# Sixteen FFN weight loads issued from GpSimd's queue, each behind a VectorE operation, in a one-core long-convolution and SwiGLU kernel

## The chip, the cores and the metric

One core of a Trainium2 chip. The metric is the device time of one execution in microseconds. The kernel before took 284.51, 283.94 and 284.5 us in three runs, a median of 284.5.

## What is computed

The reference normalises `x` (2048 rows of 640, bf16), runs a gated long convolution on it and then a SwiGLU feed-forward network (FFN), each with a residual. Cut to what matters:

```python
k_shift = sum over t of k_pad[:, t:t + S, :] * shift_k[:, 3 - t]      # 4 taps
kv = k_shift * v
y = irfft(rfft(pad(kv)) * rfft(pad(ssm_k)))[:S] + kv * ssm_D          # per channel
h = x + layernorm(x) * y
n = layernorm(h)
out = h + (silu(n @ w_gate) * (n @ w_up)) @ w_down                    # 640 -> 1728 -> 640
```

## The kernel before, in words

The 2048 positions are cut into four blocks `j` of 512, the 640 channels into two halves `c` of 320. The transform is a product with tables on TensorE (PE): block 0 uses dense tables, blocks 1 to 3 a two-stage transform whose stages are joined by shuffles, DMAs from SBUF to SBUF (`sh...` on the way there, `rs...` on the way back). VectorE (DVE) does the tap products (`kvn`, `kva`, `kvv`, line 709), the spectral products (`m1`, `m2`, `ac`, `ci`, `kf`, line 709 too) and part of the FFN's products (`gm`). ScalarE (ACT) empties PSUM. GpSimd (POOL) does twelve small powers for LayerNorm at line 839 (`nr`), and nothing else after the start.

For blocks 1 to 3 the filter `ssm_k` mostly comes in turned: a DMA transpose from DRAM (`kraw`, line 570), a store to a scratch tensor (`kst`), and a reload in another layout (`kld`), three DMAs that wait for one another; then PE's first pass (`s1K`) reads it. LayerNorm ahead of the FFN of block 0 goes: the power `nr10` on GpSimd, a product on VectorE at line 846, the normalised rows `hn` (line 853 on VectorE, line 854 on ScalarE), a transpose on PE (line 1075), a copy out of PSUM on VectorE (line 470), and then the FFN's matmuls (line 489). It is done for two halves of block 0, so `nr10` occurs twice.

The weights come in pieces: gate and up in column ranges 0, 1 and 2, each with rows 0 to 2 and 3 to 4 of five (`wg00`, `wg03`, `wg10`, ..., `wu23`), the last 64 columns of both as `gul`, and `w_down` in five pieces `wd` and one `wdl`. Each is one DMA, issued by SyncE (SP).

The order of the work is no decision of the hardware. A table, `_PLAN`, gives for each operation its engine, its place in that engine's order, planned times, and for some transfers another operation to wait for. Each engine runs its list in order; an instruction that waits holds up everything behind it on its engine. `plan()` reads the table (its last loop is quoted here), and `emit()` turns dependencies into semaphore waits. A transfer whose kind starts with "turn" is a DMA transpose, of DRAM (`kraw`) or of SBUF (`tr`, line 1067):

```python
            if o.dma[1].startswith("turn"):
                if soft is not None:
                    o.deps.setdefault(soft, 1)
                turn = o
            elif o.eng == "pool":
                if turn is not None:
                    o.deps.setdefault(turn, 1)
                soft = o
```

So, in the order of planned times, a transfer of GpSimd waits until the last transpose ahead of it has landed, and a transpose waits for the last transfer of GpSimd. In the kernel before GpSimd has no transfers, and the rule does nothing.

The plan also picks the slots of tiles that share memory. The builder of one DMA is `dma()`, whose `eng` names the queue; `load_weights()` holds `piece()`, which the diff changes; `LE` is "sp".

Of the kernel before, what the change touches and what calls it, by code (L numbers as in the profile page):

```python
# [307 lines left out]
def bass_sequential_preLN__ssm_conv_h3__swiglu_ffn__prompt_kernel(  # L308
# [14 lines left out]
    UC = [4,4,4,0]  # L323
# [29 lines left out]
    with ExitStack() as es:  # L353
# [875 lines left out]


# [10 lines left out]
    "c-rlI2UwF=+y6O9NCMf5kw6GZNC=QH0!c`KKn4T|5W*G&5kvuJt*h?VZMC(yw^ngfTlc85b+@isYg@Hit99?ufr|f|h-kmQz23Lq_pbkS^?9!6dCs`ceeV1B`<;j9x;ViIBO)T8)&s*uXnSH$3lUCI+xfEeM<;GO"  # L1241
    "39pn09`CQ7$kYCEmY3H{i+{ZKy!`w7e{x1*yY25=pJPn=hfadW@_!z<Et@}I`&;D~EWN0a{!Z!t&i$*`i_w3t{nfFAKk)g#wI{Tz<M&Md{}S)3cw-M6q(5x`_v(o7FVNBdg%#2t;{3Pp{-eHsj;DW>^8VX%{4J}0"
    "tX9ImNv(vxq1NA){!?oGWAy**TjW3g-uqX@{Ew)K@H;gT{t4w*RrJF9|L%#~we~#j=iggI<b^2h8B;vDw6-&#or!3OipYqI=!l0{$Pf9T0K|rq4n5vb=OPib_@i*7fl-UvMw4Nb58S=L#v7hYIJw|~j(nk=ia1af"
    "qCluI;Pi*57)ihz8+v3&i9%5X^wPjqj-*I|B2h53>yZ^|c9aDcW|Rh2ZdB}vo(5jHh!37A5M}Er0RR5rgAZPLP>V*fC=TghJO|peC<?`+1n?k%8H~t;5>YZzK_)>c1*IYjvca5D$bm9pWCn7=*gRAOK5|hZ%0@Y;"
    "0J%^;%w2-YQ5iCzDpZO(piZbGs)T$yqZ;s+jB1e@@Dac`J>X-6mQ<M42L8?9H4pMhgZT>4bo3f{NrD~|Sk$1ds0)lugVJJ@4ptUV)){C3#FGQ|#V~s@ng}fph$Ii<D?p=A1;kQ`s^QrPv6P}-s4qO1pq{864M7dy"
    "bw2tKe7u3)L?fVWJeq{wMem^QXc*Mrg0m}l8H2{cRR_HBffpel!U1*yfq_uKEe0Y;hiGhQDBw{AQCFi`Xb#~1Ca}u{1_gj(7@!)4LV!6LpsE0MDB%i&k`R1}z*j5ZL0}<)OA1yxU?2vtse?G9p{9np2BOy??mlQZ"
    "8U!(o2Xre@H^3zucuxeJT2bu|Ev;N?V03G~y-^R;4-JNl#sLeRA;M08RSvZEM$5q03e+FGZUD=b5JwP15&{t>!OTf8qX|42folWQ5}_OiF-L+HH4uLUWT1wc3g(OOXdnyjBLPh_@S_JFN2B*VI8H)S0o9o>TThs^"
    "J7}aB7|I1c9cTiY43<`y#SGX_L2m=r)6iTr4=n%<^nloU0j{Nx!2q-xVqFC|4@Bz#f%WJkv=(L?jJBd}p!A(EcQv41gEpZpkneD`3w;8t?T5^30k1Bgo%vw91MZs<9nV5DV5UZhtr6Wovth=K&^`maK0_a%<!BF#"
    "ejjZ|OuPzaUXRuQUd_PlbhH%Or=jc6w*}_d08wB}!-vrkbQB!~i{t1EbP`3t3}2%&=set~qXW=$2z<T+t564w8UR~4U{LN^A-w>Xx$w4_3F`a_=K26;TaAd=3;O`ZF<@N*`s@kFmBN_Tl~)L>tpt?k^eDaz{J1~`"
    "9pQ9CPZp>$AGBTvSvSDQ_rYHUpjqe9$7aZMIYj?4`V`RE3sD_{_>KTulYxOLU^fu$M*Glb5c6U5IXZ#90$wHpSK}eW<KS^JaQY6kokU+kuHQk1=h3(59AtY9{eW%)hRb1PH39p>(KqNcI)%PRXVFD;30(otTM!?A"  # L1250
    "jM#WTpvS{I5f`Teb6sGy^#^Q6!<w54T9^s(jDy<ipo4y(&ym3VaM1rCs11a+Do}Gz$Yv2Bz5v$TRdgA~w??@T*t~~sp$q6o^Z?yK57B+}GkS!6MNc5-b)c3_pvqB5iKSSEqj5OaVja%F%fL?)jJ}I*gMQY+idYBh"
    "<1zXLJw+t=13|$ph=9r18&k0l-V1*A0e)j4$|xLz)mVjNaRQFVDflzUQh+}}zW8&%SBO7F{@4!(;C-ORU>t&JNRAbF5@7x=3dBLU75`8ihUq90ABVg(cnaw28qE9zkiCaG<2#_ytAO4`KsyItgk0}IR%fB52tR{A"
# [76 lines left out]
```

## Time and profile before

| | |
|---|---|
| Median of three runs | 284.5 us (283.94 to 284.51) |
| The profiled execution | 285.35 us |
| Span of its instructions, first to last | 283.6 us |
| Mean granted TensorE clock | 0.994 |
| DMA traffic | 43.82 MB, mean 155 GB/s |
| DMAs issued by SyncE, ScalarE, GpSimd | 188, 2, 0 |

The profiled execution lies 1.75 us above its span, for what happens before the first and after the last instruction. A row of the timeline has start and length in us, engine, line, operation, what it writes and reads, its shape and a count; "SPq" is an issue by SyncE, whose length is the time of the issue and not of the transfer. In square brackets stands how long the engine had idled and what ended that. "To landing" runs from the start of the issue to the last byte. Rows of the windows view hold busy time and number of instructions by engine.

### The profile page before, as it was taken

The page shows a single profiled execution, that of the slowest core. Times are in us where ns is not written, and L with a number is a line of the kernel's source. Part 1 is how long each engine was busy: PE and PEld are TensorE (multiplying, and loading weights), DVE is VectorE, ACT ScalarE, POOL GpSimd, SP SyncE. Part 2 cuts the span into 40 slices and gives each one's busy share as a digit, 9 for nine tenths or more (in the row PEclk, how much of TensorE's full clock was granted, in tenths as well). Part 3 has the DMA queues.
Part 4 walks back from the last instruction along what each step waited for, and adds up shares of the span by engine and source line. Part 5 has one row for each costly group of instructions (what it writes and reads, how often), then busy time and mean ns, then how long its engine had stood idle before and what let it go on. Part 6 is the DMA issues. An engine that isn't in the chain of part 4 may idle for free.

```text
span 283.6 us, 4749 instructions
## 1 busy us (share of the span) xinstructions
PE 269.8 (95%) x1691; PEld 147.5 (52%) x1709; DVE 230.2 (81%) x433; ACT 196.2 (69%) x322; POOL 18.4 (6%) x21
## 2 busy tenths in 40 slices
PE   7799988799999999999999899999999999999996
PEld 2367655254445467644444477544445675444574
DVE  3997999999999999999899999999998724042414
ACT  4168988999899879959999778968899731510100
POOL 3000030200000203000001203000001010000000
PEclk9999999799999999999999999999999999999999
DMA  6987998988967547477366452763004053000003
GB/s 176 292 298 221 235 308 258 275 279 266 315 199 218 204 125 235 80 243 209 117 186 197 117 165 66 126 214 85 0 0 175 13 68 120 0 0 2 0 0 95
DMA packets 55859, 43.82 MB, mean 155 GB/s; under 512 B 20064, under 2 KB 52379, under 8 KB 55836
## 3 DMA queue, kind: packets, MB, share of 16 engines
q1 hardware_dynamic: 55690, 43.48, 52.2%
q8 instruction: 14, 0.23, 0.4%
q14 instruction: 9, 0.07, 0.1%
q10 hardware_dynamic: 146, 0.04, 0.1%
HBM read 21.88 MB, written 4.59 MB: 93 GB/s over the span
## 4 chain that ended last, share of the span: by engine, by line
PE 83%; DMA 7%; DVE 5%; issue 3%; ACT 1%; SPq 0%; DVEq 0%; ACTq 0%
PE ps L489 82%; DVE sb L709 4%; DMA sb<-in_A_k_dram 3%; DMA sb<-in_A_ssm_k_dram 2%; DMA k_nat<-sb 1%; DMA sb<-sb 1%; ACT sb L469 0%; PE ps L1075 0%; SPq L477 0%; ACT sb L1030 0%; DVE sb L470 0%; DVE sb L1167 0%; DVE sb L1034 0%; DVE sb L1101 0%; DVEq L217 0%
## 5 line engine op out<-in xcount | busy, mean ns | idle before, releaser
L489 PE MATMUL ps<-sb 128*128 128x320 bf16 (+2 forms) x1215 | 223.4, 338 | 5.0 <-issue 1.6
L709 DVE TENSOR_TENSOR sb<-sb 128x1280 bf16<-128x1280 bf16 (+4 forms) x266 | 176.5, 726 | 5.1 <-ACT sb L469 2.7
L489 PEld LDWEIGHTS ps<-sb 128*128 128x128 bf16 (+1 forms) x1233 | 119.0, 99 | 94.7 <-issue 9.0
L469 ACT ACTIVATE sb<-ps 128x640 bf16<-128x640 f32 (+2 forms) x153 | 104.9, 737 | 28.7 <-PE ps L489 23.2
L489 PE MATMUL ps<-sb,tab 128*64 128x320 bf16 (+2 forms) x432 | 55.4, 307 | 5.6 <-ACT sb L469 1.7
L1125 ACT ACTIVATE sb<-ps 128x1024 bf16<-128x1024 f32 (+2 forms) x32 | 29.3, 920 | 29.2 <-PE ps L489 28.9
L489 PEld LDWEIGHTS ps<-sb,tab 128*64 128x64 f16 (+2 forms) x432 | 25.2, 102 | 33.6 <-issue 12.6
L709 DVE TENSOR_TENSOR sb<-ps,sb 128x1024 bf16<-128x1024 f32 (+2 forms) x20 | 19.7, 1003 | 22.1 <-PE ps L489 22.1
L839 POOL TENSOR_TENSOR stt<-stt 128x2 f32<-128x2 f32 (+1 forms) x12 | 16.3, 1356 | 210.4 <-DVE stt L835 210.4
L1030 ACT ACTIVATE sb<-ps,stt 128x320 f32<-128x320 f32 x32 | 18.4, 624 | 6.3 <-PE ps L489 4.9
L1034 DVE SCALAR_TENSOR_TENSOR sb<-sb,stt 128x320 bf16<-128x320 bf16 x32 | 16.5, 545 | 3.1 <-ACT sb L1030 2.0
L873 ACT ACTIVATE sb<-sb,stt 128x640 uint8<-128x640 bf16 x16 | 13.4, 838 | 0.2
L866 ACT ACTIVATE sb<-sb 128x640 uint8<-128x640 bf16 x16 | 11.8, 738 | 0.5 <-DMA sb<-in_A_q_dram 0.4
L1167 DVE SCALAR_TENSOR_TENSOR sb<-ps,stt,sb 128x320 bf16<-128x320 f32 x8 | 4.1, 548 | 9.8 <-PE ps L489 9.8
L891 ACT ACTIVATE sb<-sb,stt 128x640 uint8<-128x640 bf16 x12 | 9.9, 829 | 0.6 <-DVE stt L886 0.2
L854 ACT ACTIVATE sb<-sb,stt 128x640 bf16<-128x640 bf16 x8 | 7.1, 916 | 0.0
L1192 DVE SCALAR_TENSOR_TENSOR sb<-ps,stt,sb 128x640 bf16<-128x640 f32 x4 | 3.3, 876 | 3.3 <-PE ps L489 3.3
L1188 ACT ACTIVATE sb<-ps,stt 128x640 bf16<-128x640 f32 x7 | 5.5, 785 | 0.0
L607 PE MATMUL ps<-sb 128*128 128x128 bf16 (+1 forms) x24 | 4.2, 282 | 0.4 <-DMA sb<-in_A_ssm_k_dram 0.4
L607 PEld LDWEIGHTS ps<-sb 128*128 128x128 bf16 (+1 forms) x24 | 2.0, 118 | 4.1 <-DMA sb<-in_A_ssm_k_dram 2.2
L853 DVE TENSOR_SCALAR sb<-sb,stt 128x640 bf16<-128x640 bf16 x8 | 3.4, 437 | 0.6 <-DMA sb<-sb 0.5
L819 DVE BATCH_NORM_STATS2 stt<-sb 128x6 f32<-128x320 bf16 x8 | 3.5, 480 | 0.0
(30 smaller groups left out, 30.3 us busy)
## 6 DMA issues: line engine op xcount, KB each, us to landing
sb<-sb SPq DMA_DIRECT2D x72, 160.0 KB, 2.6
sb<-in_A_k_dram SPq DMA_DIRECT2D x6, 560.0 KB, 4.5
sb<-in_A_v_dram SPq DMA_DIRECT2D x8, 320.0 KB, 4.0
sb<-in_A_q_dram SPq DMA_DIRECT2D x8, 320.0 KB, 4.4
sb<-cst_den SPq DMA_DIRECT2D x8, 256.0 KB, 4.3
k_nat<-sb SPq DMA_DIRECT2D x6, 320.0 KB, 4.4
sb<-k_nat SPq DMA_DIRECT2D x6, 320.0 KB, 3.0
out_dram<-sb SPq DMA_DIRECT2D x12, 160.0 KB, 2.0
```

The costliest lines, as they stand in the source:

```text
L469: fns = {"act": lambda a: a.activation(out=dst(), in_=src(), func=ACTF.Copy), "dve": lambda v: v.tensor_copy(out=dst(), in_=src())}
L489: return lambda t: t.matmul(o(), l(), r(), start=st, stop=sp)
L607: return t.transpose(B16(pt, b // 2, (b % 2) * CW + d * 128, pr), src, V(IDN, 0, pr, 0, pr))
L709: return lambda v: v.tensor_tensor(out=o(), in0=a(), in1=b_(), op=op)
L839: P.op({"pool": 1.05}, lambda g: g.tensor_tensor(out=y, in0=va, in1=stt[:, oCO + 4:oCO + 4 + hi - lo], op=ALU.pow), c1 + [(ST, "half")], c ...
L854: "act": lambda a: a.activation(out=dst(), in_=src(), func=ACTF.Identity, scale=rs(l, j, b), bias=tmv(l, j, 3)[:, b:b + 1])},
L866: P.op({"act": act_c(D) + 0.22}, lambda a, b=b, jt=jt: a.activation(out=JU(jt), in_=V(xt, b * D, D), func=ACTF.Copy, accum_out=tmv(l, j, 4 ...
L873: P.op({"act": act_c(D) + 0.3}, lambda a, b=b, jt=jt: a.activation(out=JU(jt), in_=V(xt, b * D, D), func=ACTF.Square, bias=tmv(l, j, 5)[:, ...
L891: P.op({"act": act_c(D) + 0.3}, lambda a, b=b, jt=jt: a.activation(out=JU(jt), in_=V(xt, b * D, D), func=ACTF.Square, bias=tmv(l, j, 5)[:, ...
L1030: P.op({"act": act_c(CW, True)}, lambda a, k=k, b=b, wt=wt: a.activation(out=VF(wt, CW), in_=B32(pt, k, CW), func=ACTF.Identity, scale=tmv ...
L1034: vec(dve1(CW), lambda v, b=b, wt=wt, xv=xv: v.scalar_tensor_tensor(out=xv(), in0=xv(), scalar=tmv(0, j, 5)[:, b:b + 1], in1=VF(wt, CW), o ...
L1125: P.op({"act": act_c(n)}, lambda a: a.activation(out=dst(), in_=src(), func=ACTF.Silu), rd, wr, -1000, name=f"si{j}{i}")
```

## The change

Sixteen of the twenty weight loads go from SyncE's queue to GpSimd's. Four stay on SyncE: `wg00`, `wu00`, `wg03` and `wg13`. Each of the sixteen gets one VectorE operation to wait for, from the list `PACED` (load, which of that name, VectorE operation, which of that name). The order of all other instructions on each engine is as before. The plan's table is new as a whole; the engines of the sixteen loads, their places, the transfers that some transfers wait for, the planned times and some slots of shared tiles are what differs in it.

```diff
-                dma(subs, kb, [], cells, {"0": 1020, "1": 1036, "2": 1040}.get(nm[2:3], 1041), eng=LE, after=list(more), name=nm)
+                dma(subs, kb, [], cells, {"0": 1020, "1": 1036, "2": 1040}.get(nm[2:3], 1041), eng=LE if nm in ("wg00", "wu00", "wg03", "wg13") else "pool", after=list(more), name=nm)
...
+        PACED = [
+            ('wu03', 0, 'kvn21', 0),
+            ('wg10', 0, 'kva21', 0),
+            ('wg23', 0, 'kva21', 0),
+            ('wu10', 0, 'kf102', 1),
+            ('wu13', 0, 'kvv20', 0),
+            ('gul', 0, 'kvv20', 0),
+            ('wd', 3, 'm1o102', 0),
+            ('wg20', 0, 'm1o102', 0),
+            ('wu23', 0, 'kva21', 2),
+            ('wd', 1, 'gm01', 0),
+            ('wu20', 0, 'm1a100', 0),
+            ('wd', 2, 'ac100', 1),
+            ('gul', 1, 'ci100', 0),
+            ('wd', 0, 'm2a110', 0),
+            ('wd', 4, 'ci110', 0),
+            ('wdl', 0, 'gm05', 0),
+        ]
...
+        for a_, i_, b_, k_ in PACED:
+            o, p = named[a_][i_], named[b_][k_]
+            if p not in o.deps:
+                o.deps[p] = 2
+                p.succ.append(o)
+                o.npred += 1
```

GpSimd, from the first power of block 0's second LayerNorm on. Before, the two powers `nr10` (128x2) stand next to each other, then the power of block 1 (128x4):

```order
L839 TENSOR_TENSOR stt<-stt 128x4 [waits s_pool,s_dve]
L839 TENSOR_TENSOR stt<-stt 128x2 [waits s_dve] x2
L839 TENSOR_TENSOR stt<-stt 128x4 [waits s_dve]
L839 TENSOR_TENSOR stt<-stt 128x2 [waits s_dve] x2
```

Now, with `wu03` (the first DMA; `s_d50` is the landing of the transpose `kraw20`) and `wg10` behind it:

```order
L839 TENSOR_TENSOR stt<-stt 128x4 [waits s_pool,s_dve]
L839 TENSOR_TENSOR stt<-stt 128x2 [waits s_dve]
L477 DMA sb<-in_B_w_up_dram 128x2x512 [waits s_d50]
L839 TENSOR_TENSOR stt<-stt 128x2 [waits s_dve]
L477 DMA sb<-in_B_w_gate_dram 128x3x512 [waits s_dve]
```

`wu03` has come between the two powers, and the second can only run when `wu03` has been issued. At the end of the moved loads stand the last two `wd`, the power of block 1, and `wdl`:

```order
L477 DMA sb<-in_B_w_down_dram 128x3x640 [waits s_dve]
L477 DMA sb<-in_B_w_down_dram 128x2x640 [waits s_dve]
L839 TENSOR_TENSOR stt<-stt 128x4 [waits s_dve]
L477 DMA sb<-in_B_w_down_dram 64x640 [waits s_dve]
L839 TENSOR_TENSOR stt<-stt 128x2 [waits s_dve] x2
```

SyncE at the same place, before: three shuffles, `wdl`, the transpose `kraw21`, its store `kst21`, a copy and its reload `kld21`:

```order
L477 DMA sb<-sb 32x4x640 [waits s_act] x2
L477 DMA sb<-sb 128x1x640 [waits s_d84]
L477 DMA sb<-in_B_w_down_dram 64x640
L570 DMA_TRANSPOSE sb<-in_A_ssm_k_dram 128x4x320 [waits s_d39,s_d89]
L477 DMA k_nat<-sb 128x4x320 [waits s_d94]
L477 DMA sb<-sb 128x1280 [waits s_dve]
L477 DMA sb<-k_nat 128x1280 [waits s_d87,s_d95]
```

Now, where `s_d120` is the landing of `wdl`:

```order
L477 DMA sb<-sb 32x4x640 [waits s_act] x2
L477 DMA sb<-sb 128x1x640 [waits s_d70]
L570 DMA_TRANSPOSE sb<-in_A_ssm_k_dram 128x4x320 [waits s_d39,s_d120,s_d74]
L477 DMA k_nat<-sb 128x4x320 [waits s_d78]
L477 DMA sb<-sb 128x1280 [waits s_dve]
L477 DMA sb<-k_nat 128x1280 [waits s_d79]
```

`wdl` has left SyncE's queue, and `kraw21`, which only followed it, now waits for its landing on GpSimd's side. Sixteen issues like `wdl`'s are gone from SyncE between `kraw20` and `kraw21`.

More of the change, by code (lines that the diff above doesn't have):

```diff
@@ L1228, in bass_sequential_preLN__ssm_conv_h3__swiglu_ffn__prompt_kernel @@
             block_j(j)
+        PACED = [
[16 more added lines that the diff above has]
+        ]
+        named = {}
+        for o in P.ops:
+            named.setdefault(o.name, []).append(o)
+        for a_, i_, b_, k_ in PACED:
[4 more added lines that the diff above has]
+                o.npred += 1
         if _INFO is not None:
@@ new lines @@
+    "NB}(woLqQ@AQ5N_gc&JPpfIF{S$~j~AqkQr4GM*E6H0-e9c6$-0&;*<J}UNj?+;oShzXi~!OK@C3-ohA2NSdgK~Ik&Q8bEy^>i4ELONtb7SJF93$Z8;#UmS1K_o(yh>}n;N(Gxb<U;ANG7V+I+B{SQI&zR3Wua_T"
+    "h;mT@*e*fks0}isDpZQfP&-tC+JX=5Q4Q#`p^hj5@L_rI&_Xo+fP)`+K=a_qgm@X?ISb81J-|;ZSd9bgHK-PKfVB>2EksU;I@uF-8tM!FWP=CAV7(ZPhY=Tek_Y}3qLHW)d})iS;W-U_DMejTPk1guT~H@95OoHv"
+    "^Ux~L@eUe}hQiEPG!acflVR0h=#PN27_^K=W8f+UKbephJ|IGe><AzOVGzFoJaB?Hsb~=3Q3bJAquJ;KkQ@#%Q6VB0pr`~?l}HSklLD%8V21)OCA9dUD;RXW%C`_CL~uz!Dh4uOfQ;0GpL*y;K#uyMUf_3kGz9er"
@@ new lines @@
+    "pT+{ZZBZTIk_gu00jEe{L<5Yx%B2=ozlygTYDB%!0Ep;a$U=MYupQu+1Y_OMQqc7=>H}KWgXD7XLkOOT!9y!pwt~et&=d=~HbdVG&nWO&16<UC|7wUJ0(vU2r}l6l1Mb5B%>>Ag3A`GGrh0Ikh^7OoO<=7HSZ(lR"
+    "DHE9Efaf?g2_#d%N&;a29-07H&p>m~Tr?jz&<MVD1$@&Xg1%@a___jc?uXU_0_)JHXbo5!fVQA*!0l$RT>z*TqK#-X#5)9ihIRq=`ylcnz{?HXnFq2v;Jyh3;Mr&vSegdDO+(+I_rc-@7@q}NU!qUYGPE03e}uLp"
+    "DqaDW*P+#b*K^41OtcurXP|FkZZp_e4_;vGj}M|l=rH;MSa<{-MJJFNk44|0v*;q+N29;N%zn^01Uxl*GHL=&Bm)jvfJ9r!${cuGGyyw*1Y4hgwUvm7y)hp!HURdOz}YTPU8NxXs`A_rYYF5h0W$9Z)|EpA<U_Sp"
@@ new lines @@
+    "z`Xz}&FZO;dZ?Suu<|3&mknsvd-$;lB3%aFZ$+O28hgO2{ovmr$krstz<Z#h4(&vH(U;)!L398eLnk3G;~`gLA;KeIZ4%^kGK`%-$06495aC618eM>BZ=);d4q&(pDr*U3yDK_{&Y-W+C3Fs5Mc2?x(7YKj@m3Uw"
+    "_W^oAxEV396RM^I)MFpOb`;dybl^f0`13CGYJjyJV15{6ehBctKXA7na3c>Qtpp4{gq+NWn!AN=KrOuTasg!XA-an$qwDAqx{n^C@6i+V1A2yjf|%C=TQ&mUdm#muU@6w)a2$nWa2j3;dX~WI2k0JPy#^{`E!4*g"
+    "^c4M!yx<4I7yp6?*a!Pz5+>t4pl2`O*B89eVFQl9DjbO|*oYJHmk=cj??P;R0PyAG&k+}MFc0qqHilv`4n{I8$AbX#p-6y*_!a(PScwHlgO31*wRjlt>o!>a36On=+T;7c(OZDtRX{r%Uxip7LR9BqqzJ!+A1ZH*"
@@ new lines @@
+    "@gtD$1osCJ>tm44$3LTAkPrC!J!-&I;3x~C_!)J<?_fG+U_Ks==YnTE9D>K-`QR-Fd>Mu3p<pb)q4-@q2kJ5x-Wj#PoF2fP-hlo<$o>S#<Za05b>zkmz{gh@cgBra2=((mAh-k={1sH>24L70KzkKb$qJ~{cOb)q"
+    "0n^36^SQwInSk*^;AbPSv^zv|0(722CLD_|0B6nv@8WPgHsffVfUP(gXW~M@{uyNB2~_P=@Zt>c?KHCCBzzh8cO4j*iXGUFQ?L`ea5~Pyd6<BIfLi(ym^}s20H>~)h`ZxJ?1g*4TsKU?G{7SmP!Qo$!1k|z`DcLH"
+    "C!sYF*f<K_VW)xTUjzG(d+OmJuzwt|a||%$72hwT44eag-GS=;7UkjsT#QR`1#W}e;woGXjCqcH@e6osOb1@x08ZUSWw-=J?*TKvL*=+5uEZU1J6wxva2>A40l+m1WOgPX8U&o{1sU#%nZUt*fIwf|8~1^{`r(0i"
@@ new lines @@
+    "5Dr0u@eteu^0QHYJOI}E<DqyM4n@Q92>d=8i9Y~#$${xwh;#z5UIDyU0|H}#wHn~R4hP}!z&{xvZ3ZkRVH5B;7OH}UCj%;CsE|lt&_v+53OLRL_Kd?*AU7#^8vYPj0qq%h2}%IWXW>Pj98AX_LH2C;J-iSlLq?|J"
+    "1t<+N(gbyu2>F_c7sGpfAY3I-+eP>z;9e*E1?Cba;|mxQa)^cS9!dxNn+Z>WN7o=zk=`MMF5XwXo)cygyh&v52+~aNMF0E5wgJuF%l*noPkhsS$>ezQ#Q<l(S^w`STc}2Al{}vCH9<>sc%AaHc&{h4CyKqD-bSC{"
+    "B%+^@ypg=jw}ZdPhwA&4Zz5>~S?+(!pG8_jVvw`^#`uQ^6b7{M!{oIA1`2`lh{B~l_u1}yCSY6upF*Z?qxPjepsi=vX^$Aq%tL_}>5`ypv?f*<dn<9W*KqImeV+K%k-WXS`e=Obk-GW~@LwFTD<GLd^<UusAzAHz"
@@ new lines @@
+    "n_5O&PCG>#9QcLb1M+a%F6u7Y^1yC%CGBGxhn_&MrGG*HilL=^O37sOV$5NjWAqGq9Asq9V9J@b%p1&?%u3eJtZ7Uo>m-ZH60i=lidp+u3s~9gDeMOJZgwcg&8}i|IqTVU4v$mM*}@sb3Fg*wFELLAaL5N)`#Drr"
+    "G;a()Gx!B3Lbyz@g}+vGLUK*eSI7@uA^SpF5S*>J$oY!bm$Q?*T#_xlEa6D`{Mphv`A7U}-V?45e^aneaFgIh@E$?$ke@<Qg&&9R7Yzue1^b0`6fy*3L)wJ?Eb1ew7uzID#JeT;Lq~+l!btLdqJ#3yvNO`9%Hptk"
+    "S@*D>Dw^W9;*)T!xvtBPsMRLwZ2I@~X)01UM}1Rc*Ns#sYrfQc7_m;bmw4811NoDHmDIDoC#gx4WwZpkjm>7a3+~0Q<$3YMAsL|~CC5cV=?Ai>G89G*rTSd;N%37viY1p)EcB7|_JLCaiS%Z=nNi2M%g``YL2DSR"
@@ L1299 @@
+    "MfY$26@pqZe&Z)@jqbJlubFvMpKtp_Y^_sb>-ENO;#*M=-^w+yl`Dkb`1<RPSKNvmZj~mqVoGTBgV2gSZn21d(?V}qc%$)G-2WeaXqZp"
 )
```

97 lines of the change are left out of this document (39 added, 58 removed).

## The prediction

> **What bounds the kernel now.** I read the totals first, then the chain that ended last, then busy time by stretch, because a share over the whole span hides which engine sets the pace where the change acts.
>
> ```profile
> span 283.6 us, 4749 instructions
> PE 269.8 (95%) x1691; PEld 147.5 (52%) x1709; DVE 230.2 (81%) x433; ACT 196.2 (69%) x322; POOL 18.4 (6%) x21
> ...
> PE 83%; DMA 7%; DVE 5%; issue 3%; ACT 1%; SPq 0%; DVEq 0%; ACTq 0%
> ```
>
> TensorE is busy for 95% of the span and holds 83% of the last chain. The sixteen moved loads were issued by SyncE between 55 and 100 us. The windows view for that stretch (per row: length, then busy time and count of PE, PEld, DVE, ACT, POOL, then granted clock, DMA share, GB/s) says more:
>
> ```profile
> 55.00:60.00 5.00, 4.69 (x43) 2.52 (x43) 4.65 (x15) 4.89 (x8) 1.20 (x1) 0.85 0.92 278
> 60.00:75.00 15.00, 14.71 (x95) 7.34 (x95) 14.86 (x24) 14.57 (x24) 0.00 (x0) 1.00 0.90 278
> 75.00:90.00 15.00, 14.94 (x93) 7.58 (x94) 15.00 (x26) 13.43 (x23) 0.00 (x0) 1.00 0.69 224
> 90.00:107.00 17.00, 16.54 (x117) 9.40 (x118) 16.76 (x41) 14.06 (x25) 1.51 (x1) 1.00 0.59 183
> ```
>
> From 55 to 107 us PE lacks only 0.31 + 0.29 + 0.06 + 0.46 = 1.12 us of full time, and VectorE 0.35 + 0.14 + 0 + 0.24 = 0.73 us. Two engines are full at once, each with a fixed order. So little can be won here, and what either loses by a new wait is not made good later. The waits of PE's weight loads from 55 to 165 us (total, times, longest) name a transfer once:
>
> ```profile
> PEld ps L489 <- DMA sb<-sb: 0.4, 1, 0.4
> ```
>
> **The change part by part.** It takes sixteen issues off SyncE, puts them on GpSimd, and adds two kinds of waits: sixteen on VectorE (written in the diff) and, through the plan's rule at the end of `plan()`, waits between GpSimd's loads and SyncE's transposes. Issue time saved on SyncE (0.43 us for the first load, row below) is worth nothing by itself: no transfer that SyncE issues later stands in PE's way for more than the 0.4 us above. The VectorE gates cost nothing either, since most end about when SyncE issued the load before; the loads keep their order of need. What costs is where GpSimd, in order as well, meets the two other waits.
>
> Step 1: `wu03`, the first load on GpSimd. It must wait until the transpose `kraw20` has landed, and behind it on GpSimd stands the second LayerNorm power of block 0 (L839, `nr10`), for which VectorE waits. From the timeline (start, length, engine) and the issues view (the transpose issued at 52.78 landed 3.9 us later):
>
> ```profile
> 52.78 1.59 SPq L570 DMA_TRANSPOSE sb<-in_A_ssm_k_dram  x1
> 55.04 0.43 SPq L477 DMA_DIRECT2D sb<-in_B_w_up_dram  x1
> 52.93 0.96 POOL L839 TENSOR_TENSOR stt<-stt 128x2 f32<-128x2 f32 x1 [14.40 <-DVE stt L835]
> 56.11 1.20 POOL L839 TENSOR_TENSOR stt<-stt 128x2 f32<-128x2 f32 x1 [2.22 <-DVE stt L835]
> 155.08 3.00 POOL L839 TENSOR_TENSOR stt<-stt 128x4 f32<-128x4 f32 x1 [42.73 <-DVE stt L835]
> 57.94 0.15 DVE L846 TENSOR_TENSOR stt<-stt 128x2 f32<-128x2 f32 x1
> 58.74 0.44 DVE L853 TENSOR_SCALAR sb<-sb,stt 128x640 bf16<-128x640 bf16 x1
> 60.53 0.82 DVE L470 COPY sb<-ps 128x1280 bf16<-128x1280 bf16 x1
> 59.78 0.72 PE L1075 MATMUL ps<-sb 128*128 128x128 bf16 x10
> 61.41 1.52 PEld L489 LDWEIGHTS ps<-sb 128*128 128x128 bf16 x11 [0.31 <-DVE sb L470]
> ...
> sb<-in_A_ssm_k_dram SPq DMA_TRANSPOSE x1, 3.9
> ```
>
> The transpose and all that SyncE issues ahead of it stay where they were, so it lands at 52.78 + 3.9 = 56.7 again. Then GpSimd issues `wu03` in a time X. The trace of before has no DMA issue by GpSimd, so X is bounded: 0.43 us below (SyncE's issue of this very load), 3.00 us above (its longest instruction, at 155.08). I take X = 1.0, nearest to GpSimd's own two rows in this stretch, 0.96 and 1.20. The power then starts at 56.7 + 0.05 + 1.0 + 0.05 = 57.8 instead of 56.11, takes its 1.20 and ends at 59.0; L846 follows at 59.04 instead of 57.94. Before, 57.94 − 57.31 = 0.63 us of other VectorE work hid the power's end; that cover is used up. VectorE is late by 1.1 = X + 0.1, and so are the queued instructions behind L846, down to the copy at 60.53, for which PE's weight load at 61.41, the FFN's, had waited already (its row names L470), so PE has nothing to spare there. **Term 1: S = 1.1 us**, between 0.5 (X = 0.43) and 3.1 (X = 3.00). `wu03` itself is hidden: issued near 56.8 and landing 4.0 us later (first row below), it is there at 60.8; its first matmuls (the piece of the chain at 62.19) then start at 63.3.
>
> ```profile
> sb<-in_B_w_up_dram SPq DMA_DIRECT2D x1, 256.0 KB, 4.0
> ...
> 62.19 9.48 PE ps L489 x55
> ```
>
> The Trainium skill, "DMA: Bandwidth & Descriptors", section "Specifications", gives a first byte after about 1 us for a DMA from GpSimd and 0.6 us for one from SyncE. No run here shows it yet; by it X would be an estimated 0.43 + 0.4 = 0.83 and the sum below 2.2 us, not 2.5.
>
> The other GpSimd instruction in the stretch, the power at 92.55, gets the load `wd` (rows 11 and 12) ahead of it. It ended at 94.06 and its reader on ScalarE started at 98.09, so 4 us hide it.
>
> ```profile
> 92.55 1.51 POOL L839 TENSOR_TENSOR stt<-stt 128x4 f32<-128x4 f32 x1 [35.23 <-DVE stt L835]
> 98.09 1.13 ACT L1030 ACTIVATE sb<-ps,stt 128x320 f32<-128x320 f32 x2
> ```
>
> Step 2: `wdl`, the last load, gated by the FFN product at 97.74 (L709 from PSUM, ends 98.95). The transpose `kraw21`, which merely followed it on SyncE, must now wait until `wdl` has landed. Behind `kraw21` stand its store, the reload `kld21`, and PE's first pass over it at 111.33. Timeline and landing times:
>
> ```profile
> 97.74 1.21 DVE L709 TENSOR_TENSOR sb<-ps,sb 128x1024 bf16<-128x1024 f32 x1
> 99.80 0.60 SPq L477 DMA_DIRECT2D sb<-in_B_w_down_dram  x1
> 100.50 1.37 SPq L570 DMA_TRANSPOSE sb<-in_A_ssm_k_dram  x1
> 105.53 0.38 SPq L477 DMA_DIRECT2D k_nat<-sb  x1
> 107.96 0.35 SPq L477 DMA_DIRECT2D sb<-k_nat  x1
> 111.33 0.23 PEld L489 LDWEIGHTS ps<-sb,tab 128*128 128x128 f16 x2
> ...
> sb<-in_B_w_down_dram SPq DMA_DIRECT2D x1, 80.0 KB, 3.0
> sb<-k_nat SPq DMA_DIRECT2D x1, 320.0 KB, 2.9
> ```
>
> The gate ends at 98.95 + S = 100.05. `wdl` lands L later: 3.0 before, of which 0.60 was the issue, so L = 3.0 + (1.0 − 0.6) = 3.4, that is 103.5. `kraw21` starts there and not at 100.50: 3.0 late. It is a chain of latencies (100.50, 105.53, 107.96, landing 110.86), so `kld21` lands near 113.9. PE wants it at 111.33 + 1.1 = 112.4. **Term 2: 1.4 us** (before it had 0.47 to spare). In general the sum is S + L − 2.0 = 2X + 0.5.
>
> Sum: 1.1 + 1.4 = **2.5 us**. Against the profiled execution, 283.6 of span and 1.75 around it (285.35), that is 287.85; the median of the runs shown is 0.85 lower than that execution, so 284.5 + 2.5 = **287.0**. With X from 0.43 to 1.9, 285.9 to 288.8.
>
> **The rivals.**
> - *Only the first wait counts*: `kraw21` took 5.0 us to land while weights and shuffles ran beside it, others of its kind 3.4. Gaining 1.6 there pays term 2.
>
> ```profile
> sb<-in_A_ssm_k_dram SPq DMA_TRANSPOSE x1, 5.0
> ...
> DMA to landing us min/median/max: 3.4/4.7/5.4
> ```
>
>  The sum is S = 1.1: 285.6. For it: DMA traffic falls after `wdl`. Against: the chain's other two transfers stay. 16%.
> - *GpSimd issues slowly.* GpSimd's instructions took 0.70 us with VectorE idle (226.67: VectorE busy 0.04) and 3.00 with VectorE full.
>
> ```profile
> 226.67:227.36 0.69, 0.69 (x7) 0.50 (x6) 0.04 (x1) 0.69 (x2) 0.69 (x1) 1.00 0.00 0
> 155.08:158.08 3.00, 2.95 (x17) 1.56 (x16) 3.00 (x6) 1.62 (x3) 3.00 (x1) 1.00 0.21 65
> ...
> 67.76 1.14 SPq L477 DMA_DIRECT2D sb<-in_B_w_up_dram  x2
> ...
> sb<-in_B_w_up_dram SPq DMA_DIRECT2D x1, 480.0 KB, 6.6
> ...
> 82.48 1.89 PE L489 MATMUL ps<-sb 128*128 128x512 bf16 x8
> ```
>
>  From `wu13` (issued at 67.76) six issues lead to `wu20`, which takes 6.6 us to land and is wanted by the sixth of the eight matmuls of the row at 82.48, near 83.6. 67.76 + 6X + 6.6 passes 83.6 + S from X = 1.9 on. At X = 2.2: S = 2.3, `wu20` 1.7 late, L = 4.6, in all 2.3 + 1.7 + 4.6 − 2.0 = 6.6: 291. 12%. The Trainium skill, "SBUF — State Buffer", section "SBUF: two separate sides", speaks for this rival and so against the change: while VectorE runs a two-port operation, GpSimd cannot write the descriptors of its DMAs. By its section "Who interferes with whom", copies and scalar operations between SBUF tiles are such operations and L709's kind is not; of the rows here that is L853 alone, 0.44 us, by which X would stay an estimated 1.0 + 0.44 at most and the sum 3.4.
> - *The clock drops.* After PE had been busy 0.68 of 2 us, its granted clock fell to 0.50:
>
> ```profile
> 50.00:52.00 2.00, 0.68 (x8) 0.29 (x8) 2.00 (x5) 1.56 (x4) 0.00 (x0) 1.00 0.71 255
> 54.00:56.00 2.00, 1.71 (x11) 0.56 (x10) 2.00 (x10) 1.79 (x4) 0.00 (x0) 0.50 1.18 326
> ```
>
>  A drop of 4 us to half speed after one of the two new pauses costs 2 us more: 289.0. Each pause is under 1.5 us. 6%.
> - *Faster.* SyncE's shuffles no longer stand behind weights. If `kraw20` landed before 55.0 (so that X + 56.11's power fits ahead of 57.94) and `wdl` by 101, both waits would be covered, and of PE's 1.12 us of gaps perhaps 0.8 would close: 283.7. Against: nothing ahead of `kraw20` moves, and one wait of 0.4 us names a transfer. 7%.
> - *No change*: the gates end where SyncE issued anyway, and both added waits hide in slack that the trace does not show: 284.5. 9%.
>
> **How the numbers follow.** The forecast has 50%, the rivals 16, 12, 6, 7 and 9. A difference of 0.2% is about what a measurement of this kernel can tell from none. Slower: 50 + 16 + 12 + 6 = 84%; same 9%; faster 7%. The range goes from no change, 284.4, to the sum at X = 2.0 (S 2.1, `wu20` 0.7 late, L 4.4: 5.2), 289.7; outside are the faster case and the upper part of slow issues, some 15%.
>
> **What would show it.** In the timeline after: `wu03`'s issue on GpSimd at 56.7, L839 behind it near 57.8, VectorE idle ahead of L846 for about 1 us "until POOL"; `kraw21` near 103.5, and PE waiting over 1 us for `sb<-k_nat` near 112. Wrong it is if L839 still starts at 56.1, if PE's wait at 112 is missing, or if X is over 1.9 and the up-projection near 84 waits for its weights.

## The result, and the profile after

The changed kernel took **288.44 us** (287.23 to 290.24, four runs) against 284.5 us for the kernel before on the same chip: a ratio of 1.014, 95% interval 1.0097 to 1.0182. In a later series on one chip it was 287.34 us (ten runs) against 284.75 (27 runs): 1.0085, interval 1.0053 to 1.0116. So the loss is 2.4 to 4 us; the prediction said 2.5, at 287.0. The ratios here and below leave out executions over 1.5% above the fastest of their kernel; of the swapped kernel that is four of six, of the fourteen one and of the kernel with a brake two, the profiled one among them each time, so a wait in these three profiles is relied on only where another kernel's profile shows it too.

The page of the changed kernel, its totals and two groups of GpSimd's issues (busy time in us and mean ns of one, then the idle time before them):

```profile
span 286.2 us, 4747 instructions
PE 269.6 (94%) x1691; PEld 147.4 (52%) x1709; DVE 230.5 (81%) x433; ACT 196.0 (69%) x322; POOL 31.2 (11%) x37
...
L477 POOL DMA_DIRECT2D sb<-in_B_w_up_dram x6 | 4.7, 792 | 11.3 <-DVE sb L709 7.2
L477 POOL DMA_DIRECT2D sb<-in_B_w_down_dram x6 | 4.4, 728 | 13.9 <-DVE sb L709 9.1
```

PE's work is the same, 269.6 us against 269.8; the span has grown by 2.6 us of waiting. An issue by GpSimd takes 0.73 to 0.79 us on average in these two groups. Where PE waits, the windows of the changed kernel tell (length; then busy time of PE, PEld, DVE, ACT, POOL; clock, DMA share, GB/s):

```profile
55.00:60.00 5.00, 3.50 (x34) 1.83 (x30) 3.05 (x8) 3.47 (x7) 2.16 (x3) 0.97 0.91 226
60.00:75.00 15.00, 13.83 (x89) 6.90 (x92) 14.86 (x23) 13.76 (x22) 7.66 (x11) 1.00 0.98 298
```

From 55 to 60 us PE has 3.50 us of work instead of 4.69 and VectorE 3.05 instead of 4.65: the first wait. (The clock was 0.97 there instead of 0.85, so PE's busy time alone overstates what it lost.) From 60 to 75 PE has 13.83 instead of 14.71, while the DMA engines are busier (0.98 instead of 0.90): this was not foreseen. GpSimd and VectorE at the first place, from the timelines of the changed kernel:

```profile
56.58 0.89 POOL L477 DMA_DIRECT2D sb<-in_B_w_up_dram  x1 [4.05 <-DMA sb<-in_A_ssm_k_dram]
57.50 0.72 POOL L839 TENSOR_TENSOR stt<-stt 128x2 f32<-128x2 f32 x1
...
58.25 0.16 DVE L846 TENSOR_TENSOR stt<-stt 128x2 f32<-128x2 f32 x1 [1.38 <-POOL stt L839]
```

`wu03` waits 4.05 us for the transpose `kraw20`, holds GpSimd for 0.89, and the power `nr10` behind it ends at 58.22; VectorE has stood still for 1.38 us "until POOL". This execution had come to 47 us some 1.4 us ahead of the profiled one of before (a repeat of the kernel before was 0.6 us ahead there too, so such a lead is partly chance). The lead only makes VectorE's wait longer, since the power starts when `wu03` has been issued. That L846 starts at 58.25 and not at the 59.04 of the forecast comes mostly from the power, which took 0.72 us and not 1.20.

The waits of the changed kernel between 55 and 75 us (total, times, longest) and, below, the piece of its chain of waits that leads to PE's stop near 72:

```profile
PEld ps L1075 <- DVE sb L853: 1.7, 1, 1.7
DVE stt L846 <- POOL stt L839: 1.4, 1, 1.4
PEld ps L489 <- DMA sb<-sb: 1.1, 1, 1.1
```

```profile
58.99 6.97 DMA k_nat<-sb
...
67.07 5.39 DMA sb<-sb
...
72.50 0.46 PE ps L489 x4
```

The store `kst20` took 6.97 us to land where it took 4.9 (5.5 in the repeat of the kernel before), and the shuffle `shK11G0` 5.39 where its like took 3.0 (both from the issues view of before); PE's own loading of weights (PEld in the rows) stood 1.1 us for that shuffle, PE itself 0.8. SyncE issued the store 2.2 us earlier than before, and it landed no earlier. At the last load the timelines of SyncE and GpSimd and the issues view of the changed kernel show:

```profile
100.11 0.59 POOL L477 DMA_DIRECT2D sb<-in_B_w_down_dram  x1 [4.40 <-DVE sb L709]
...
103.24 1.38 SPq L570 DMA_TRANSPOSE sb<-in_A_ssm_k_dram  x1
...
sb<-in_A_ssm_k_dram SPq DMA_TRANSPOSE x1, 3.5
```

`kraw21` starts 2.7 us late, at 103.24 (forecast 103.5), but lands in 3.5 us and not in 5.0, and PE does not wait for `sb<-k_nat` near 112 in this execution.

### The profile page after: what moved, and what is told of

Read it like the earlier page. It is cut to its first block, busy times and chain, and to the rows that moved or that the text cites. A ratio compares the mean times of both kernels' runs of the same rounds, so it can differ in the third digit from the quotient of the medians.

```text
span 286.2 us, 4747 instructions
## 1 busy us (share of the span) xinstructions
PE 269.6 (94%) x1691; PEld 147.4 (52%) x1709; DVE 230.5 (81%) x433; ACT 196.0 (69%) x322; POOL 31.2 (11%) x37
## 4 chain that ended last, share of the span: by engine, by line
PE 73%; DMA 13%; SPq 4%; DVE 3%; issue 3%; ACT 3%; ACTq 0%; DVEq 0%
PE ps L489 72%; DMA k_nat<-sb 4%; DMA sb<-sb 4%; SPq L477 4%; DVE sb L709 3%; ACT sb L469 2%; DMA sb<-in_A_ssm_k_dram 2%; DMA sb<-in_A_v_dram 2%; DMA sb<-k_nat 1%; DMA out_dram<-sb 1%; ACT sb L1030 1%; DVE sb L470 0%; PE ps L1075 0%; DVE sb L1167 0%; DVE sb L1101 0%
## 5 line engine op out<-in xcount | busy, mean ns | idle before, releaser
L709 DVE TENSOR_TENSOR sb<-sb 128x1280 bf16<-128x1280 bf16 (+4 forms) x266 | 176.7, 725 | 4.4 <-ACT sb L469 2.3
L709 DVE TENSOR_TENSOR sb<-ps,sb 128x1024 bf16<-128x1024 f32 (+2 forms) x20 | 19.7, 1003 | 22.9 <-PE ps L489 22.9
L477 POOL DMA_DIRECT2D sb<-in_B_w_up_dram x6 | 4.7, 792 | 11.3 <-DVE sb L709 7.2
L477 POOL DMA_DIRECT2D sb<-in_B_w_down_dram x6 | 4.4, 728 | 13.9 <-DVE sb L709 9.1
```

What stands on the lines that cost most here:

```text
L477: fns = [(lambda g, d=d, s=s: g.dma_start(d(), s())) for d, s in subs]
L709: return lambda v: v.tensor_tensor(out=o(), in0=a(), in1=b_(), op=op)
```

## Experiments

Two theories. **The waits (A)**: the loss is what the two added waits cost, `nr10` behind `wu03`, and `kraw21` behind `wdl`. **The shared queues (B)**: loads on GpSimd's queue are no longer behind SyncE's transfers in one order but run beside them, and slow the ones that PE or VectorE wants next. Edits are against the changed kernel, cut to what matters. A kernel that puts loads back has a list `BACK`: each load in it returns to its old place in SyncE's order, without its gate. The excess of a kernel is (ratio − 1) times the median of before on its chip.

**Before again.** No edit.

> The kernel before, looked at a second time, for what two executions of one program differ by ahead of 55 us, where the change touches nothing. In the profile of after, VectorE reached the tap product kvn21 at 47.14 us, in that of before at 48.51. If that lead of 1.36 us is chance, this profile also lies somewhere between 46.8 and 49; if every profile of the kernel before has it at 48.4 to 48.6, the change does something ahead of its own loads. Total 284.5, within 1.

It took 284.2 us, span 282.4. At 50 us it was 0.6 us ahead of the first profiled execution, so shifts of that size at that point are chance.

**The power ahead of the load.**

```diff
+    q = P.order["pool"]
+    i = [o.name for o in q].index("wu03")
+    q[i], q[i + 1] = q[i + 1], q[i]
```

> The change with one thing undone: on GpSimd the second power of block 0 (nr10) stands ahead of wu03 again. Theory A (added waits: wu03's wait for kraw20 holds the power, and with it VectorE): L846 is no longer late, the profile's PE pause of 1.4 us ahead of L1075 near 60 goes, 1.5 to 2 us faster than the change: 286.4 to 286.9. Theory B (sharing: the loads on a queue of their own slow SyncE's transfers between 59 and 75 us, and that sets PE's times): what is won at 60 is lost again near 72, where shK11G0 lands; under 0.7 us faster, 287.8 to 288.4.

292.23 us (six runs, before 284.08); ratio 1.0139 (1.0053 to 1.0225), from two of them. Its profiled execution took 291.59. Timeline of GpSimd, waits, windows and issues of the swapped kernel:

```profile
55.57 1.20 POOL L839 TENSOR_TENSOR stt<-stt 128x2 f32<-128x2 f32 x1 [2.22 <-DVE stt L835]
57.15 0.89 POOL L477 DMA_DIRECT2D sb<-in_B_w_up_dram  x1 [0.38 <-DMA sb<-in_A_ssm_k_dram]
...
DVE sb L709 <- DMA sb<-in_A_v_dram: 3.1, 1, 3.1
...
70.00:75.00 5.00, 1.32 (x10) 0.54 (x8) 4.86 (x8) 0.52 (x2) 2.47 (x5) 0.78 1.00 299
75.00:80.00 5.00, 4.41 (x19) 1.68 (x16) 3.53 (x8) 2.89 (x5) 2.22 (x3) 0.54 1.06 376
...
k_nat<-sb SPq DMA_DIRECT2D x1, 320.0 KB, 9.8
```

The first wait is gone, `nr10` runs at 55.57, and no row names L846. But the kernel is not faster: a new wait has come, VectorE's for `vin20` (a load of `v`; the row names `in_A_v`), 3.1 us, `kst20` takes 9.8 us, and PE stops for 3.7 and 0.6 us at shuffles. After these stops the granted clock is 0.54 for 5 us. Of the 1.5 to 2 us that theory A alone had forecast as a gain nothing shows.

**`wdl` back.**

```diff
+BACK = [("wdl", 0)]
```

> The change with wdl alone back on SyncE's queue ahead of kraw21, without its VectorE gate; kraw21 then waits for a load that has landed at 97.6. By the second step of the prediction (kraw21's wait holds PE for 1.4 us) it is 1.4 us faster than the change: 287.0. By the profile of after, where kraw21 landed in 3.45 us and not 5.0 and PE did not wait, it is the same: 288.4 within 0.5.

287.39 us; ratio 1.0101 (1.0046 to 1.0155), an excess of 2.9 us. VectorE's wait at L846 is there (1.6 us). Against 2.4 and 4.0 for the whole change this doesn't tell what `wdl` costs; the test of it alone, below, does.

**Eleven back.**

```diff
+BACK = [("wg10", 0), ("wg23", 0), ("wu10", 0), ("wu13", 0), ("gul", 0), ("wd", 3),
+        ("wg20", 0), ("wu23", 0), ("wd", 1), ("wu20", 0), ("wd", 2)]
```

> The change with the eleven loads from wg10 to the third wd (GpSimd's from 59 to 75 us) back on SyncE's queue in their old places, without gates; wu03, the second gul, two wd and wdl stay on GpSimd. Theory A: the power still stands behind wu03, nothing is won but noise: 288.0 to 288.6. Theory B: kst20 and shK11G0 take 4.9 and 3.0 us to land again and not 7.0 and 5.4, PE's pause of 0.95 us near 72.5 goes: 1 to 1.5 us faster, 286.9 to 287.4.

288.25 us; ratio 1.0134 (1.0087 to 1.0182). `kst20` lands in 4.5 us and the stop near 72 is gone, as theory B had it, and yet the time is no better than with all sixteen. Theory B's gain does not show either. In the profiled execution the wait at L846 was only 0.4 us (VectorE came late to it, after 1.7 us of waiting for `in_A_k` near 49 us, where it was 0.7 before), so I can't say from its rows where the 3.8 us lie; the last experiment but one takes this up.

**The changed kernel again**, as the base for the next three.

> The changed kernel as it is, for a base on the same chip as the next three. Both theories: 288.4 us as measured, 287.2 to 290.2, and again the transposes kraw21 near 103 us, landing in 3.4 to 3.6 us.

287.34 us; 1.0085. Its profiled execution (287.21 us) loses its time in other places than the first one. Waits and SyncE's timeline:

```profile
DVE stt L846 <- POOL stt L839: 1.7, 1, 1.7
...
PEld ps L489 <- DMA sb<-k_nat: 2.0, 1, 2.0
PE ps L489 <- DMA sb<-k_nat: 1.7, 1, 1.7
...
104.34 1.39 SPq L570 DMA_TRANSPOSE sb<-in_A_ssm_k_dram  x1
```

Here `kst20` landed in 5.3 us, the shuffles were issued 2.3 us earlier than before and came in time, and there is no stop near 72. But `wdl` took 4.9 us to land (99.36 to 104.29), `kraw21` started at 104.34, and PEld waited 2.0 us for the reload, PE itself 1.7: the second term of the prediction, as it was forecast. One kernel, two executions, two places, nearly the same sum.

**Only `wu03` on GpSimd.**

```diff
+BACK = [("wg10", 0), ("wg23", 0), ("wu10", 0), ("wu13", 0), ("gul", 0), ("wd", 3),
+        ("wg20", 0), ("wu23", 0), ("wd", 1), ("wu20", 0), ("wd", 2), ("gul", 1),
+        ("wd", 0), ("wd", 4), ("wdl", 0)]
```

> Only wu03 is issued by GpSimd; the other fifteen are back at their old places on SyncE. Theory of the waits: the first wait alone, S = 1.1 to 1.5 us, so 285.3 to 285.7 us with before at 284.2; nr10 near 57.6, L846 about 1.5 us late against the ops of 55 us, and the same shift kept to the end. Theory of the shared queues: also 285.3 to 285.7, since a single load beside SyncE's is little traffic; kst20 lands in under 5 us and PE does not stop at 72. If it is 284.4 or less, the first wait is covered by something later, and neither theory has its price right.

286.47 us (twelve runs); ratio 1.0063 (1.0034 to 1.0092), **+1.8 us** (1.0 to 2.6). Timelines of GpSimd and VectorE:

```profile
57.15 0.87 POOL L477 DMA_DIRECT2D sb<-in_B_w_up_dram  x1 [3.29 <-DMA sb<-in_A_ssm_k_dram]
58.05 0.72 POOL L839 TENSOR_TENSOR stt<-stt 128x2 f32<-128x2 f32 x1
...
58.80 0.16 DVE L846 TENSOR_TENSOR stt<-stt 128x2 f32<-128x2 f32 x1 [1.22 <-POOL stt L839]
```

This is the prediction's first step by itself: one load on GpSimd, VectorE idle for 1.22 us ahead of L846, and the time up by 1.8. PE does not stop near 72, as expected, but `kst20` took 6.5 us where under 5 was expected, though all loads from `wg10` on are SyncE's: its time to land varies for other reasons too.

**Only `wdl` on GpSimd.**

```diff
+BACK = [("wu03", 0), ("wg10", 0), ("wg23", 0), ("wu10", 0), ("wu13", 0), ("gul", 0),
+        ("wd", 3), ("wg20", 0), ("wu23", 0), ("wd", 1), ("wu20", 0), ("wd", 2),
+        ("gul", 1), ("wd", 0), ("wd", 4)]
```

> Only wdl is issued by GpSimd, behind its gate; the other fifteen are back on SyncE. The prediction's second term: kraw21 starts near 102.4 us, 1.9 us late, lands in 5.0, and PE waits 1.4 us near 112: 285.6 us with before at 284.2. The second term hidden: kraw21 lands in 3.4 us, no wait at 112, and only the later transposes behind it cost up to 0.5 us: 284.2 to 284.7.

285.12 us; ratio 1.0001 (0.9973 to 1.0029), **0.0 us** (−0.8 to +0.8). SyncE's timeline, issues and waits:

```profile
102.19 1.40 SPq L570 DMA_TRANSPOSE sb<-in_A_ssm_k_dram  x1
...
sb<-in_A_ssm_k_dram SPq DMA_TRANSPOSE x1, 3.4
...
PEld ps L489 <- DMA sb<-k_nat: 0.4, 1, 0.4
```

`kraw21` is 1.7 us late and lands in 3.4 us; PEld waits 0.4 us, PE itself not at all. This kernel has the changed kernel's new table, so the table itself costs nothing that shows. Over all profiles the time to land goes with the wait: where `kraw21` starts when `wdl` has landed it took 3.4 to 3.5 us five times and 4.2 and 4.3 twice; where `wdl` is issued by SyncE 0.7 us ahead of it, 4.7 to 5.4 six times (3.5 once, in the fourteen, which run 7 us late there). So the wait mostly gives back some 1.6 us of what it takes.

**Fourteen**, all but `wu03` and `wdl`, so that neither added wait is left.

```diff
+BACK = [("wu03", 0), ("wdl", 0)]
```

> wu03 and wdl are back on SyncE, so that neither nr10 nor kraw21 has a new wait; the other fourteen loads stay on GpSimd behind their VectorE operations. Theory of the waits: nothing is left of the loss, 284.0 to 284.6 us. Theory of the shared queues: the loads from 57 to 70 us run beside SyncE's store and reload of K and its shuffles, kst20 takes 7 us or more to land, shK11G0 5 us or more, PE stops near 72 us for 1 to 5 us: 285.5 to 290 us.

290.47 us (six runs); ratio 1.0166 (1.011 to 1.0223), **+4.7 us** (3.1 to 6.4). Its waits from 55 to 75 us, in a profiled execution of 292.52 us:

```profile
PEld ps L489 <- DMA sb<-sb: 5.2, 1, 5.2
...
DVE sb L709 <- DMA sb<-in_A_v_dram: 2.8, 1, 2.8
```

With neither of the two added waits the change costs more than with both. Theory A would have had nothing left here; this is B's cost. No engine waits for one of the sixteen loads in this profile, so it is not that the gates bring them too late.

**Three** of the fourteen, issued at 58.25, 59.17 and 61.91 us.

```diff
+BACK = [("wu03", 0), ("wu13", 0), ("gul", 0), ("wd", 3), ("wg20", 0), ("wu23", 0),
+        ("wd", 1), ("wu20", 0), ("wd", 2), ("gul", 1), ("wd", 0), ("wd", 4), ("wdl", 0)]
```

> Only wg10, wg23 and wu10 are on GpSimd, behind their VectorE operations; the other thirteen loads are back on SyncE, so that no new wait is left at nr10 or kraw21. Theory of the shared queues: these three alone hold up vin20 and kst20 (8 us or more from issue to landing, against 3.39 and 4.86 before), kld20 lands after 71 us, PE stops at 72 for 1 us or more: 286 to 290.5 us with before at 284.7, most of the loss of the fourteen. Theory of the waits: 284.3 to 285.1. If kst20 is slow and the time is not, the loss of the fourteen comes from the eleven other loads.

285.73 us (before 284.12); ratio 1.0055 (1.0019 to 1.0091), **+1.6 us** (0.5 to 2.6). Waits and issues:

```profile
DVE sb L709 <- DMA sb<-in_A_v_dram: 1.5, 1, 1.5
...
sb<-in_A_v_dram SPq DMA_DIRECT2D x1, 320.0 KB, 7.1
k_nat<-sb SPq DMA_DIRECT2D x1, 320.0 KB, 7.4
```

`vin20` lands in 7.1 us where it took 3.4, `kst20` in 7.4 where it took 4.9, and VectorE, which between 55 and 75 us had not waited for a transfer in before, waits 1.5 us for `vin20`. I had expected the cost at PE near 72 and by `kst20`; it is VectorE by `vin20` (PE stood 0.4 us for a shuffle), and it is a third of the fourteen's loss, not most of it. With the lateness of `vin20` goes the order of issue. The first fence has SyncE's timeline and issues of before, where `wg10` follows `vin20`; the second SyncE and GpSimd of the three, the third those of the changed kernel:

```profile
59.49 0.59 SPq L477 DMA_DIRECT2D sb<-in_A_v_dram  x1
60.12 0.63 SPq L477 DMA_DIRECT2D sb<-in_B_w_gate_dram  x1
...
sb<-in_A_v_dram SPq DMA_DIRECT2D x1, 320.0 KB, 3.4
k_nat<-sb SPq DMA_DIRECT2D x1, 320.0 KB, 4.9
```

```profile
58.61 0.59 SPq L477 DMA_DIRECT2D sb<-in_A_v_dram  x1
...
58.25 1.65 POOL L477 DMA_DIRECT2D sb<-in_B_w_gate_dram  x2 [1.69 <-DVE sb L709]
```

```profile
58.36 0.59 SPq L477 DMA_DIRECT2D sb<-in_A_v_dram  x1
...
59.45 1.49 POOL L477 DMA_DIRECT2D sb<-in_B_w_gate_dram  x2 [1.24 <-DVE sb L709]
```

With the three, the gate lets `wg10` go 0.36 us ahead of `vin20`; in the changed kernel `wg10` follows 1.09 us behind it, because `nr10`'s wait has made VectorE, and with it the gate, late. In all four profiles in which `wg10` went first (the swapped kernel, the fourteen, the three, and the one with a brake below) `vin20` took 7.1 to 8.6 us and VectorE waited 1.5 to 3.1 us for it; in none of the others did it wait. Where `wg10` followed on GpSimd 1.1 to 1.4 us later, `vin20` took 4.8 to 6.2 us (three profiles); where it followed on SyncE, 3.4 to 5.6 (seven).

**All sixteen, with the power ahead of `wu03` and a brake**: `wg23` waits until `kst20` has landed.

```diff
-            ('wg23', 0, 'kva21', 0),
+            ('wg23', 0, 'kst20', 0),
...
+    q[i], q[i + 1] = q[i + 1], q[i]
```

> All sixteen stay on GpSimd. nr10 goes ahead of wu03, as in the swapped kernel, and the load wg23 waits until the store kst20 has landed, and with it, in GpSimd's order, everything behind it. Theory of the shared queues: it is who runs beside kst20 that counts and not the issuing engine; kst20 takes under 7 us, kld20 lands by 70, no stop of PE at 72 over 0.5 us, and with both waits gone 284.3 to 286 us, at least 2 us under the changed kernel of 287.3. If loads from GpSimd cost in themselves, it stays at 287 or over. The wait can cost something of its own where wu10 lands after 73 us, when PE wants it.

289.04 us; ratio 1.0167 (1.0118 to 1.0215): a miss. Waits of its profiled execution, of 296.11 us:

```profile
PEld ps L489 <- DMA sb<-sb: 3.6, 2, 3.5
...
DVE sb L709 <- DMA sb<-in_A_v_dram: 1.6, 1, 1.6
```

`wg10` was again issued ahead of `vin20` (59.01 against 59.38), which took 7.1 us, and `kst20` 7.5. When the brake opened at 67.5, six loads went out by 72.4, beside the shuffles `shK11G1` and `shK11G0`, issued at 67.95 and 68.59, which took 5.9 and 6.1 us. The brake has moved the burst to where the shuffles are. Here a wait on one urgent transfer did not protect the next.

**Eleven back, with the power ahead of `wu03`.** The list of the eleven above, and the swap.

> The eleven loads from wg10 to the third wd are back on SyncE; nr10 goes ahead of wu03; on GpSimd stay wu03, the second gul, two of wd and wdl, behind their gates. The kernel without the swap took 288.25 us. If what it lost came from the wait of nr10 behind wu03 and from nothing else, this takes 284.3 to 285.3 us with before at 284.7. If the loads gul, wd and wdl cost something of their own (kraw21's wait with the later transposes behind it), 286 to 287.

285.35 us; ratio 1.0054 (1.0022 to 1.0085), **+1.5 us**. The swap that gained nothing with all sixteen takes the excess from 3.8 to 1.5 us here, where the burst is away. That is the first wait's 1.8 again, within the intervals, though the eleven's own profile showed only 0.4 of it. Of the 1.5 us that remain the waits of PE from 55 to 75 us show about half:

```profile
PE ps L489 <- DMA sb<-in_B_w_up_dram: 0.5, 1, 0.5
...
PE ps L489 <- DMA sb<-sb: 0.3, 1, 0.3
```

`wu03`, issued at 56.98 instead of 55.04, is itself late now that LayerNorm isn't. The wait for a shuffle comes behind `kst20`, which took 7.3 us here with `wg10`, `wg23` and `wu10` on SyncE; why is open. The rest I can't place.

**Late eleven**, the counterpart of the three.

```diff
+BACK = [("wu03", 0), ("wg10", 0), ("wg23", 0), ("wu10", 0), ("wdl", 0)]
```

> wu03, wg10, wg23, wu10 and wdl are back on SyncE; the eleven loads from wu13 to the fourth wd, issued from 66 us on, stay on GpSimd behind their VectorE operations. The counterpart of the three alone (285.7 us with before at 284.1). Theory of the shared queues, with the cost at the shuffles shK11G1 and shK11G0: wu13, gul and two of wd and wg20 are issued within 2 us of them, the shuffles take over 4.5 us to land where they took 2.9 and 3.0, PE stops at 72 for 1 us or more, and of the fourteen's loss of 4.7 us some 2.5 to 4 are here: 286.6 to 288.5 us. If the loss of the fourteen needs both groups together (the three hold up kst20, the eleven then meet the late shuffles), this one costs under 1 us, 284.1 to 285.1, with the shuffles landing as before.

286.66 us (before 283.51); ratio 1.0108 (1.0066 to 1.015), **+3.1 us** (1.9 to 4.2). GpSimd's timeline, SyncE's issues (the two shuffles and their median time to land) and PE's timeline:

```profile
65.54 1.78 POOL L477 DMA_DIRECT2D sb<-in_B_w_up_dram  x2 [8.64 <-DVE sb L709]
...
66.79 1.19 SPq L477 DMA_DIRECT2D sb<-sb  x2
...
sb<-sb SPq DMA_DIRECT2D x2, 160.0 KB, 4.6
...
71.06 0.73 PE L489 MATMUL ps<-sb,tab 128*64 128x320 bf16 x8 [1.00 <-DMA sb<-sb]
72.43 0.46 PE L489 MATMUL ps<-sb,tab 128*64 128x320 bf16 x4 [0.64 <-DMA sb<-sb]
```

Before, SyncE issued the two shuffles and then, at 67.76, `wu13` and `gul` behind them:

```profile
66.52 1.19 SPq L477 DMA_DIRECT2D sb<-sb  x2
...
sb<-sb SPq DMA_DIRECT2D x2, 160.0 KB, 3.0
```

The shuffles took 3.0 us and landed first. Now GpSimd issues `wu13` and `gul` from 65.54 on, the shuffles take 4.6, and PE stops twice, for 1.00 and 0.64 us. Over all fourteen profiles the median of the two shuffles is 3.0 to 3.7 us where `wu13` stands behind them in SyncE's queue (seven), and 3.7 to 6.0 where GpSimd issues it (seven). `kst20` separates less: 4.5 to 7.3 us with `wg10` on SyncE, 5.3 to 9.8 with it on GpSimd.

1.6 for the three and 3.1 for the eleven make the 4.7 of the fourteen; each has an interval of 1 us or more to either side, so that the sum comes out exactly is chance. PE's two stops are 1.6 of the 3.1; the rest is not placed.

## Why the prediction was right, and where not

**Step 1 (`wu03` ahead of `nr10`): right.** X was forecast at 1.0 and is 0.87 to 0.89 us; the sixteen issues lie between 0.59 and 0.9. Alone the step costs 1.8 us (1.0 to 2.6) where 1.1 was forecast, which lies inside the interval; VectorE stood 1.2 to 1.7 us at L846 in four of the five profiles with this wait (0.4 in the other). Two parts of the working were off in opposite directions: `wu03` starts 0.29 us after `kraw20` has landed (56.86 to 57.15 in the kernel with `wu03` alone), not 0.05, and the power takes 0.72 and not 1.20, with VectorE idle beside it. That `wu03` itself would be in time holds as long as LayerNorm is late. The estimate of 0.83 us for X from the first-byte times of the Trainium skill, "DMA: Bandwidth & Descriptors", section "Specifications", came near the rows; the first byte itself no row shows. The Trainium skill, "SBUF — State Buffer", section "Who interferes with whom", by which L709's kind of operation does not keep GpSimd from its DMAs, agrees with the rows: the issues took 0.73 to 0.79 us on average beside a full VectorE. The rival in which GpSimd issues slowly is out, and so is that of the clock: its mean was 0.994 in the changed kernel's profile, as before.

**Step 2 (`kraw21` behind `wdl`): the delay right, its price mostly not.** The start at 103.24 and 104.34 was forecast at 103.5. Forecast at 1.4 us, it costs 0.0 ± 0.8 alone. The part of the rival "only the first wait counts" that speaks of `kraw21` was the right reading: behind a landed `wdl` the transpose takes 3.4 us and not 5.0. In the first profile PE's wait at 112 is missing, which the prediction itself had named as a sign of being wrong. In the other of two profiled executions of the whole change, in which `wdl` itself was slow (4.9 us), PEld did wait 2.0 us there, and PE 1.7. Why `wdl` was slow then stays open.

**The step that failed** is the one that priced the move between queues at nothing: "The VectorE gates cost nothing either, since most end about when SyncE issued the load before; the loads keep their order of need." The gates do not end there: `wg10` was issued 0.63 us behind `vin20` before and 0.36 us ahead of it with the three, `wu13` 1.24 us behind the first shuffle before and 1.25 us ahead of it with the late eleven. The order of need was kept on each queue and lost between them. On SyncE's queue a weight load stood behind `vin20` and the shuffles; on GpSimd's it runs beside or ahead of them, at about the same traffic in all (278 GB/s before and 298 after from 60 to 75 us). The urgent transfer lands later, and the loads, which have time, gain little: `wg10` landed at 63.8 with the three and at 65.7 in the changed kernel, against 64.0 before. That term is 4.7 us without the two waits: 1.6 with the three, where VectorE waits for `vin20`, and 3.1 with the eleven, where PE stops at the shuffles for 1.6. The Trainium skill, "DMA: Bandwidth & Descriptors", section "Issuing engines are not separate DMA queues", says that transfers run on the same sixteen DMA engines and interleave whichever engine has started them, and that the only gain is the issue time. The later landings fit that; what the interleaving costs is the term that the prediction left out. No run has `wg10` ahead of `vin20` in one queue, or a load on a third engine's, so whether the second queue matters or only the earlier issue stays open.

**Why the total came out near all the same.** By luck. The terms don't add: 1.8 + 0.0 + 4.7 = 6.5, and the whole change costs 2.4 in the same series. With `wu03` on GpSimd VectorE is late by 1.2 to 1.7 us, so the gate of `wg10` opens behind `vin20`'s issue and not ahead of it, and the wait for `in_A_v` (1.5 to 3.1 us in the four kernels without the first wait in which GpSimd issues `wg10`) is missing in both profiles of the changed kernel. The first wait is thus a brake that saves a part of what the sharing would cost; the three alone, where that wait for `in_A_v` is the main loss, put it near 1.6 us. That this is the reason is read from these rows and not shown by a run of its own. The swap's two faces fit it (it gained 2.3 us with the eleven back and nothing with them on GpSimd); how the whole 4.1 us is made up was not measured part by part. The forecast of 287.0 was thus near for partly wrong reasons: its first term was real, its second usually was not, and a third was missing.

No version here beats the kernel before; the nearest is `wdl` alone on GpSimd, at 1.0001.

## What to carry to other kernels

Before loads are moved to another engine's queue, look at what stood ahead of them in the old one: there the order is also a priority, and here the transfers that PE or VectorE wanted next lost it. An issue put ahead of a small operation that others wait for, on an engine that runs its list in order, costs its wait and its issue time, and it is cheap to look for: list what stands behind each moved instruction. And test removals in pairs: here each half of the cause, taken away alone, brought no gain.

## What was not expected of the hardware

- `vin20` (320 KB) landed 3.4 us after its issue in both profiles of before, 3.4 to 6.2 us after it in the other eight in which the load `wg10` of 384 KB was issued behind it, and 7.1 to 8.6 us after it in the four in which GpSimd issued that load up to 0.4 us ahead of it.
- The power of 128x2 on GpSimd took 1.20 us beside a busy VectorE and 0.72 while VectorE waited for it.
- The same DMA transpose landed in 3.4 to 4.3 us when it waited for `wdl` first and in 4.7 to 5.4, in six of seven profiles, when it was issued 0.7 us behind it.
- After PE had been busy 1.32 of 5 us (70 to 75 us in the swapped kernel), its granted clock was 0.54 for the next 5 us.
